# Local attention with global keys feeding a four-expert attention layer: global keys in place, finer VectorE steps, searched order

## The chip, the cores and the metric

One core of one Trainium2 chip. The metric is the device time in microseconds (us) of one execution; lower is better. The core has TensorE (PE in the profile, its weight loads PEld), VectorE (DVE), ScalarE (ACT), GpSimd (POOL) and SyncE (SP), which here only issues transfers. Every engine works through its own list of instructions in order and waits on semaphores for the others.

## The reference

Two layers follow each other, for 4 batches of 768 positions. The first is attention with 8 heads of 64 columns: a position sees the 8 global keys (positions 0 to 7) and the last 96 positions, with a bias that falls linearly with the distance. The second gives each position to 2 of 4 experts, and each expert is a causal attention head of its own.

```python
scores = scale * (q @ k.T)
is_global = pos[None, :] < 8
is_local = (rel >= 0) & (rel < 96)
dist = where(is_global & ~is_local, 96.0, abs(rel))
scores = where(is_global | is_local, scores - slopes * dist, -1e9)
x = softmax(scores) @ v            # 8 heads side by side: (4, 768, 512)

logits = x @ w_gate                # 4 experts, the best 2 are kept
w = softmax over the 2 kept logits
for e in range(4):
    a = softmax(causal(scale * (x @ wq[e]) @ (x @ wk[e]).T))
    out += w[e] * (a @ (x @ wv[e]) @ wo[e])
```

## The kernel before

**Tiling.** The work is cut into 24 row tiles ("units" u) of 128 positions: 4 batches b of 6 tiles ri. `unit(u)` adds some 35 stages per tile to a planner. R = 4 copies of most buffers go round.

**Stages of one tile.** Three loads (ldq, ldk, ldv, 256 KB each, line 537) fill `raw`. POOL casts q and k to 16 bits (cq, ck) and v into `V1` (cv). PE transposes q and k into PSUM (tq, line 554), and DVE copies them out to `qkT` (eq). For each half hf of the heads: PE forms the scores against the tile's own 128 keys and against the tile before, there for the first 96 queries only (s0, s1, line 583); ACT takes the exponential (x0, x1, line 590); the mask and bias are multiplied in on DVE or POOL (m0, m1, line 595); PE multiplies with the values (z0, z1, lines 601 to 609), whose 65th column of ones gives the sum; DVE takes its reciprocal into `rall` (line 616) and scales (line 617), both in one stage n0, n1. Then the transposed x (tx, line 649, and ex) goes through the expert weights: pq (queries and keys, line 659) and pv (values and gate, line 665), evacuated by eqk and ev. The gate is xr on ACT and wr on DVE, one stage of three instructions: the largest values `mx` (line 683), `wr` (684), and the reciprocal `zi` (686). The expert scores s2 (line 700), exponentials x2 (704), the causal cut af on POOL (712), the products y2 (724), then n2 on DVE, one stage of three instructions: reciprocal (730), weight `cw` (731), scaling (733). Then tz, ez, po (line 749), eo and the store so (758).

**Global keys before.** Once per batch POOL copies the 8 global keys of each head into a zeroed matrix `KG` (line 566, eight small copies), and builds `VG`, the global values times their bias factor (lines 436 and 439), from eight small loads (line 485). For each tile but the first of a batch, PE forms all heads' global scores in one product (sg, line 637, 4 products), ACT takes the exponential (xg, line 641), and z begins with one product of 260 columns against `VG` (line 601).

**The order.** `Stream` is a list planner that runs when the program is built. Each stage has a key, a function, the engines that could do it with a length each, the stages it follows, a rank and, for PE, a kind of PSUM slot: "s" (2 slots of two banks) or "w" (4 slots of one bank). `run()` takes at each step the stage and engine with the earliest start, ties going to the lower rank (5.0 × u plus a number per stage); a stage's second engine counts as 0.25 us later. A PSUM slot is taken in turn: stage n waits for the one that used the slot n places before. A change between products on 64 and 128 rows counts 0.1 us. The instructions are issued in the order found, so the list of each engine, SP's queue of transfers too, is fixed.

**The end.** A count of sums within a safe range is loaded as a flag (line 795), and every engine tests it (line 796): if a sum was out of range, `general_path`, a slow exact version, runs. In the usual case it is passed by. `preferred_fallthrough_block=False` places the usual case right behind the test, with a branch over the general path after it; instructions of line 828 are the program's closing waits.

Of the kernel before, what the change touches and what calls it, by code (L numbers as in the profile page):

```python
# [15 lines left out]
HUGE = 1.0e30  # L16
# [3 lines left out]
PACE = 5.0  # L20
# [219 lines left out]
class Stream:  # L240
# [4 lines left out]
    def __init__(self, kinds):  # L245
        self.free = {"PE": 0.0, "ACT": 0.0, "DVE": 0.0, "POOL": 0.0, "DMA": 0.0}
        self.tail = {"PE": 0.22, "ACT": 0.13, "DVE": 0.13, "POOL": 0.15, "DMA": 2.0}
        self.kinds = {k: (n, []) for k, n in kinds.items()}
        self.rows = False
        self.ops, self.done = {}, {}  # L250

    def add(self, key, fn, engines, after=(), rank=0.0, kind=None, until=()):


        assert key not in self.ops, key
        self.ops[key] = (fn, engines, tuple(after), rank, kind, tuple(until))

    def turn(self, e, kind):

        return 0.1 if e == "PE" and (kind == "s") != self.rows else 0.0  # L260

    def ready(self, key):
        fn, engines, after, rank, kind, until = self.ops[key]
# [5 lines left out]
        if kind:  # L269
# [4 lines left out]
            n, taken = self.kinds[kind]  # L274
            if len(taken) >= n:
                for a in taken[-n]:
                    if a not in self.done:
                        return None
                    t = max(t, self.done[a])
        return t  # L280

    def run(self):
        left = dict.fromkeys(self.ops)
        while left:
            best = None
            for key in left:
# [9 lines left out]
            start, key, e, length = best[3:]  # L296
            fn, engines, after, rank, kind, until = self.ops[key]
            if kind:
                self.kinds[kind][1].append(until)
            if e == "PE":  # L300
                self.rows = kind == "s"
# [7 lines left out]
def kernel(  # L309
# [18 lines left out]
    NL = N_G * H  # L328
# [504 lines left out]
```

## Time and profile before

| | us |
|---|---|
| median of 3 runs | 180.56 (180.41 to 185.12) |
| the profiled execution | 180.74 |
| its span, first to last instruction | 179.0 |
| mean granted TensorE clock | 0.953 |

The profile is one execution. Its page has the busy time of each engine, the span in 40 slices (of 4.475 us here), the chain of work that ended last, followed back from the last instruction, and groups of instructions with the time their engine was idle before them. A releaser is what ended an idle time. A record's length reaches to the acknowledged write, so the next independent instruction of an engine can start before it ends: the distance between two starts is what an instruction costs its engine.

### The profile page before, as it was taken

The numbers are of one execution on the slowest core, as the hardware profiler recorded it, in microseconds if no ns is written. First come the engines' busy times: TensorE is split into PE (matmuls) and PEld (weight loads), VectorE is DVE, ScalarE is ACT, GpSimd is POOL, SyncE is SP. The second block draws the span as 40 slices with busy tenths as digits, with TensorE's granted clock in tenths as the row PEclk, the third lists the DMA queues.
The fourth block names the chain that finished last, engine by engine and source line by source line (L and its number), as shares of the span: only waits on it lengthen the run. The fifth ranks groups of instructions, "written<-read, shape, count | busy, mean of one in ns | idle before, by whom it ended". The sixth has DMA issues, their size and how long they took to land.

```text
span 179.0 us, 5965 instructions
## 1 busy us (share of the span) xinstructions
PE 139.7 (78%) x2366; PEld 109.7 (61%) x2366; DVE 138.6 (77%) x438; ACT 110.2 (62%) x203; POOL 93.3 (52%) x169
## 2 busy tenths in 40 slices
PE   0447697499897889899999998987799987997510
PEld 0236585377775767678677876765697666774300
DVE  7554867978989699998989899879996897956500
ACT  3904138277675798546988567497568893279410
POOL 7566854764867448824957186899501650112000
PEclk9999669999999999999999999999999999999855
DMA  5996995999799599979899999910101031011120
GB/s 125 297 176 183 257 214 147 211 231 222 177 218 233 149 232 230 242 165 243 200 221 277 219 227 250 230 63 5 59 4 62 0 121 59 4 59 61 61 70 9
DMA packets 80693, 27.80 MB, mean 155 GB/s; under 512 B 75793, under 2 KB 77329, under 8 KB 80657
## 3 DMA queue, kind: packets, MB, share of 16 engines
q1 hardware_dynamic: 80656, 27.34, 67.6%
q8 instruction: 20, 0.33, 0.8%
q14 instruction: 17, 0.13, 0.3%
HBM read 21.05 MB, written 6.29 MB: 153 GB/s over the span
## 4 chain that ended last, share of the span: by engine, by line
DVE 44%; PE 34%; DMA 6%; ACT 4%; issue 3%; SPq 3%; ACTq 0%; DVEq 0%
DVE A L595 10%; PE pq L659 8%; DVE x L617 5%; DVE cw L731 5%; DVE qkT L347 5%; DVE z L733 4%; PE po L749 4%; PE pv L665 4%; DMA raw<-in_v_dram 4%; PE z L724 3%; DVE QK L347 3%; PE s L700 3%; PE tx L649 3%; DMA w<-in_moe_wv_dram 2%; SPq L537 2%
## 5 line engine op out<-in xcount | busy, mean ns | idle before, releaser
L704 ACT ACTIVATE A<-s 128x1024 f16<-128x1024 f32 (+1 forms) x48 | 42.2, 923 | 11.6 <-PE s L700 11.1
L590 ACT ACTIVATE A<-sc 128x896 f16<-128x896 f32 (+1 forms) x48 | 40.1, 870 | 3.1 <-PE sc L583 2.7
L347 POOL CAST qk<-raw 128x512 f16<-128x512 f32 x47 | 30.9, 670 | 15.8 <-DMA raw<-in_k_dram 8.0
L712 POOL TENSOR_SCALAR_AFFINE_SELECT A<-A 128x512 f16<-128x512 f16 x24 | 15.9, 661 | 36.0 <-ACT A L704 32.4
L595 DVE TENSOR_TENSOR A<-A,M 128x896 f16<-128x896 f16 (+1 forms) x37 | 26.1, 719 | 2.8 <-ACT A L590 2.6
L659 PE MATMUL pq<-xT,wqk 128*128 128x128 f16 x384 | 27.0, 227 | 0.4 <-DVE xT L347 0.2
L659 PEld LDWEIGHTS <-wqk 128*128 128x128 f16 x384 | 24.2, 102 | 2.1 <-issue 0.4
L595 POOL TENSOR_TENSOR A<-A,M 128x896 f16<-128x896 f16 (+1 forms) x11 | 19.9, 1806 | 5.3 <-ACT A L590 4.9
L617 DVE TENSOR_TENSOR x<-z,rall 128x256 f16<-128x256 f32 x48 | 20.4, 425 | 1.6
L347 POOL CAST V<-raw 128x512 f16<-128x512 f32 x24 | 15.3, 642 | 11.7 <-PE z L609 8.3
L554 PE MATMUL tq<-ident,qk 128*128 128x128 f16 x192 | 16.1, 230 | 5.3 <-POOL qk L347 4.9
L347 DVE CAST QK<-pq 128x512 f16<-128x512 f32 x21 | 14.4, 686 | 6.9 <-PE pq L659 6.7
L606 PE MATMUL z<-V,A 128*128 128x65 f16 x192 | 17.5, 197 | 2.6 <-DVE A L595 1.6
L347 ACT COPY o_sb<-po 128x512 f32<-128x512 f32 x18 | 10.6, 588 | 12.9 <-PE po L749 8.9
L347 ACT CAST V<-pv 128x256 f16<-128x256 f32 x23 | 8.6, 376 | 15.5 <-PE pv L665 15.4
L749 PE MATMUL po<-wo,zT 128*128 128x512 f16 x48 | 14.9, 393 | 4.0 <-DVE zT L347 3.9
L347 DVE COPY qkT<-tq 128x1024 f16<-128x1024 f16 x24 | 16.3, 684 | 2.1 <-PE tq L554 1.9
L606 PEld LDWEIGHTS <-A 128*128 128x128 f16 x192 | 14.3, 100 | 6.0 <-DVE A L595 2.6
L700 PE MATMUL s<-QK 64*128 64x128 f16 x336 | 15.3, 218 | 1.7 <-ACT A L590 1.1
L583 PE MATMUL sc<-qkT 64*128 64x128 f16 x192 | 14.6, 223 | 2.5 <-ACT A L590 1.2
L554 PEld LDWEIGHTS <-qk 128*128 128x128 f16 x192 | 12.4, 103 | 6.4 <-POOL qk L347 5.1
L665 PE MATMUL pv<-wvg,xT 128*128 128x264 f16 x96 | 15.5, 286 | 1.0 <-DVE wvg L347 1.0
(75 smaller groups left out, 263.5 us busy)
## 6 DMA issues: line engine op xcount, KB each, us to landing
raw<-in_q_dram SPq DMA_DIRECT2D x24, 256.0 KB
raw<-in_k_dram SPq DMA_DIRECT2D x24, 256.0 KB
raw<-in_v_dram SPq DMA_DIRECT2D x24, 256.0 KB
out_dram<-o_sb SPq DMA_DIRECT2D x24, 256.0 KB
w<-in_moe_wq_dram SPq DMA_DIRECT2D x1, 512.0 KB
w<-in_moe_wk_dram SPq DMA_DIRECT2D x1, 512.0 KB
w<-in_moe_wv_dram SPq DMA_DIRECT2D x1, 512.0 KB
wo<-in_moe_wo_dram SPq DMA_DIRECT2D x1, 512.0 KB
```

Source lines behind the costliest of these rows:

```text
L347: act.copy(o, i) if e == "ACT" else (dve if e == "DVE" else pool).tensor_copy(o, i)
L554: nc.tensor.transpose(ps[:, s, p, :], qk16[u % 3][:, s, 2 * p:2 * p + 2, :], ident[:, :])
L590: act.activation(A1[(2 * u + hf) % (2 * R)][:, :, :, 0:w], T.pop(("s", u, hf))[:, :, :, 0:w], func=Exp, scale=scale1)
L595: eng[e].tensor_tensor(a, a, M[:, hf, :, :, :] if ri else M0[:, hf, :, :, :], op=Alu.mult)
L606: mm(z[:, h % 4, :], lhsT=a[:, par, pr, 0:P], rhs=V1[u % (R + 1)][:, h, 0:DV], start=not ri, stop=not ri)
L617: dve.tensor_tensor(x16[i][:, 256 * hf:256 * hf + 256].rearrange("p (h d) -> p h d", d=Dh), z[:, :, 0:Dh], r.unsqueeze(2).to_broadcast([P, ...
L659: mm(ps[:, j, :], lhsT=wqk[:, ko, j, :], rhs=xT[i][:, ko, :], start=(ko == 0), stop=(ko == nko - 1))
L665: mm(ps[:, :], lhsT=xT[i][:, ko, :], rhs=wvg[:, ko, :], start=(ko == 0), stop=(ko == nko - 1))
L700: mm(sc[:, par, n, :], lhsT=QK2[b % 2][L, ki, 2 + p2, :], rhs=QK2[b % 2][L, ri, p2, :], start=True, stop=True)
L704: act.activation(A2[i][:, :, 4 * ch:4 * ch + m, :], T.pop(("s2", u, ch))[:, :, 0:m, :], func=Exp, scale=scale2)
L712: pool.affine_select(out=A2[i][:, :, 0:2, :], in_=A2[i][:, :, 0:2, :], pattern=[[0, 2], [0, 2], [1, P]], channel_multiplier=-1, base=0, co ...
L749: mm(ps[:, :], lhsT=zT[i][:, p2, :], rhs=wo[:, p2, :], start=(p2 == 0), stop=(p2 == E // 2 - 1))
```

## The change

- **Global keys in place.** A query of tile ri sees at most 95 positions back, so of the tile before it the keys 0 to 7 are never local. After tile u's own scores are done, its keys 0 to 7 in `qkT` are overwritten with the batch's global keys (kp, a small copy on POOL or DVE from the saved `KG`), and after its z products its values 0 to 7 in `V1` with the global values (vp, a transfer in SP's queue from the saved `VG`). The next tile then finds the global keys in the tile before it. The mask of the tile before covers 128 queries instead of 96, with the global distance put in by one more minimum (d1). The matrix `KG` with zeros, the products sg, the exponential xg, the eight loads, the building of `VG` and the `VG` product of z are gone. s of tile u + 1 follows kp of tile u, and z follows vp. `V1` has 4 copies instead of 5.
- **Small VectorE steps as own stages.** n0 becomes r0 and n0, n1 becomes r1 and n1; wr becomes mx, wr and zi; n2 becomes rz, cw and n2.
- **PSUM.** A stage takes any free slot, the one free the longest, and buffers are named by slot.
- **Ranks.** Cost is start + an extra per stage for its second engine (`OTHER`) + 0.000376 × rank, with searched ranks per stage (`RANK`) and for the weight loads (`W_RANK`).
- **The end.** The test has no preferred block, and one hint instruction per engine marks the branch as likely taken.

```diff
+PACE, ALPHA, TURN = 6.00622, 0.000375979, 0.1
+OTHER = {"m0": 3.12, "m1": 3.35, "eqk": 1.71, "ev": 14.02, "eo": 5.29, "kg": -15.22, "kp": 7.23}
+RANK = {
+    "ldq": 3.09, "ldk": -1.4103, "ldv": 10.549, "cq": 15.151, "ck": -10.082, "cv": -4.5336,
...
+W_RANK = -47.481, 2.337, 16.829, -53.198, 17.758
...
-            n, taken = self.kinds[kind]
-            if len(taken) >= n:
-                for a in taken[-n]:
-                    if a not in self.done:
-                        return None
-                    t = max(t, self.done[a])
+            free = [(max([self.done[a] for a in r], default=0.0), n)
+                    for n, r in enumerate(self.kinds[kind]) if all(a in self.done for a in r)]
+            if not free:
+                return None
+            when, self.slot = min(free)
+            t = max(t, when)
...
-                for n, (e, length) in enumerate(self.ops[key][1].items()):
-                    start = max(t, self.free[e] + self.turn(e, self.ops[key][4]))
-                    c = (start + (0.25 if n else 0.0), self.ops[key][3], n, start, key, e, length)
-                    if best is None or c[:3] < best[:3]:
-                        best = c
+                for n, (e, length) in enumerate(engines.items()):
+                    turn = TURN if e == "PE" and rows != self.rows else 0.0
+                    start = max(t, self.free[e] + turn)
+                    c = start + OTHER.get(stage, 0.0) * n + ALPHA * rank
+                    if best is None or c < best[0]:
+                        best = c, start, key, e, length, self.slot
...
+    st.add("d1", dmin(d[:, P:2 * P], d[:, P:2 * P]), {"DVE": 0.35}, ["mask", "dg"], rank=-16.0)
...
-        add("cv", lambda e: copy(e, V1[u % (R + 1)][:, :, 0:Dh], raw[i][:, 2, :, :]),
-            {"POOL": 0.6}, ["ldv", ("z0", u - R), ("z1", u - R), c("V1one")], 1.5)
+        add("cv", lambda e: copy(e, V1[i][:, :, 0:Dh], raw[i][:, 2, :, :]), {"POOL": 0.6},
+            ["ldv", c("V1one")] + [(n, u - R + a) for a in range(2) for n in ("z0", "z1")])
...
+            add("kg", lambda e: copy(e, KG[b % 2][:, :, :], qkT[i][:, 1, :, 0:N_G]), {"POOL": 0.12, "DVE": 0.1},
+                ["eq"] + [("kp", w) for w in range(u - 2 * n_rt, u - n_rt)])
+            add("vg", lambda e: copy(e, VG[b % 2][:, :, :], V1[i][0:N_G, :, :]), {"POOL": 0.55},
+                ["cv"] + [("vp", w) for w in range(u - 2 * n_rt, u - n_rt)])
...
-                            o = sc[:, par, pr, P:P + N_L] if prev else sc[:, par, pr, 0:P]
-                            mm(o, lhsT=kt[L, 1, p, :],
-                               rhs=qkT[i][L, 0, p, 0:N_L] if prev else qkT[i][L, 0, p, :],
+                            mm(sc[:, par, pr, prev * P:(prev + 1) * P], lhsT=kt, rhs=qkT[i][L, 0, p, :],
                                start=True, stop=True)
...
-                if ri:
-                    mm(z[:, :, :], lhsT=ag[i][:, :], rhs=VG[:, b, 4 * hf:4 * hf + 4, :],
-                       start=True, stop=False)
...
+            add(f"s{hf}", s1, {"PE": 0.24 if ri else 0.13}, ["eq"] + ([("kp", u - 1)] if ri else []),
+                None, "s", [f"x{hf}"], True)
...
+            add(f"z{hf}", z1, {"PE": 0.25 if ri else 0.13}, [f"m{hf}", "cv"] + ([("vp", u - 1)] if ri else []),
+                None, "w", [f"r{hf}", f"n{hf}"])
+            add(f"r{hf}", lambda e, hf=hf, r1=r1: dve.reciprocal(r1, T["z", u, hf][:, :, Dh]), {"DVE": 0.09},
+                [f"z{hf}"])
...
+        if ri < n_rt - 1:
+            add("kp", lambda e: copy(e, qkT[i][:, 1, :, 0:N_G], KG[b % 2][:, :, :]), {"POOL": 0.12, "DVE": 0.1},
+                [("kg", b * n_rt), "s0", "s1"])
+            add("vp", lambda e: nc.sync.dma_start(V1[i][0:N_G, :, :], VG[b % 2][:, :, :]), {"DMA": 0.1},
+                [("vg", b * n_rt), "z0", "z1"])
...
+        add("mx", lambda e: dve.max(mx[i][:, :], T["pv", u][:, lg0:lg0 + 2 * E]), {"DVE": 0.1}, ["pv", ("wr", u - R)])
...
+        add("zi", lambda e: dve.reciprocal(zi[i][:, :], zall[:, u:u + 1]), {"DVE": 0.08}, ["wr", ("cw", u - R)])
...
+        add("rz", lambda e: dve.reciprocal(r2, T["z2", u][:, :, Hd]), {"DVE": 0.09}, ["y2"])
...
+    st.add("hint", lambda e: tc.mark_branch_hint_location("general", "LikelyTaken", engines=engines),
+           {"DVE": 0.0}, [("y2", last)], PACE * NU + 30.0)
...
-    with tc.If(n_good < P * NU * (H + E + 1), preferred_fallthrough_block=False):
+    with tc.If(n_good < P * NU * (H + E + 1), label="general"):
```

## Rows read from the trace of the kernel before

**Rows 1.** Page: busy time by engine; rate in 40 slices; chain's shares.
```profile
PE 139.7 (78%) x2366; PEld 109.7 (61%) x2366; DVE 138.6 (77%) x438; ACT 110.2 (62%) x203; POOL 93.3 (52%) x169
...
GB/s 125 297 176 183 257 214 147 211 231 222 177 218 233 149 232 230 242 165 243 200 221 277 219 227 250 230 63 5 59 4 62 0 121 59 4 59 61 61 70 9
...
DVE 44%; PE 34%; DMA 6%; ACT 4%; issue 3%; SPq 3%; ACTq 0%; DVEq 0%
```

**Rows 2.** Busy us by stretch: PE, PEld, DVE, ACT, POOL; clock, DMA, GB/s.
```profile
18.00:25.00 7.00, 5.49 (x55) 4.63 (x52) 5.12 (x18) 1.82 (x4) 5.10 (x8) 0.56 1.15 244
40.00:158.00 118.00, 105.72 (x1894) 84.83 (x1888) 104.21 (x323) 81.75 (x146) 65.50 (x104) 1.00 0.70 156
80.00:100.00 20.00, 18.93 (x362) 15.31 (x361) 17.93 (x56) 16.51 (x26) 12.29 (x24) 1.00 1.05 237
158.00:171.00 13.00, 9.63 (x161) 6.06 (x158) 6.72 (x32) 9.18 (x16) 1.92 (x3) 0.92 0.17 62
```

**Rows 3.** Groups by form: busy us, mean ns of one | idle before.
```profile
L704 ACT ACTIVATE A<-s 128x1024 f16<-128x1024 f32 x36 | 35.9, 1030 | 9.8 <-PE s L700 9.4
L590 ACT ACTIVATE A<-sc 128x896 f16<-128x896 f32 x40 | 35.6, 924 | 3.1 <-PE sc L583 2.7
...
L595 POOL TENSOR_TENSOR A<-A,M 128x896 f16<-128x896 f16 x9 | 17.6, 1952 | 5.2 <-ACT A L590 4.9
...
L601 PE MATMUL z<-VG,ag 128*128 128x260 f16 x40 | 11.2, 281 | 2.1 <-DVE QK L347 1.2 <-ACT ag L641 0.5 <-DVE x L617 0.2
...
L731 DVE SCALAR_TENSOR_TENSOR cw<-wr,zi,rall 128x4 f32<-128x4 f32 x24 | 10.0, 415 | 0.9
...
L637 PE MATMUL sg<-qkT,KG 128*128 128x128 f16 x80 | 7.8, 219 | 1.1 <-DVE qkT L347 1.1
```

**Rows 4.** Chain that ended last, one piece: start us, us, what.
```profile
134.68 0.89 PE pq L659 x16
```

**Rows 5.** Instructions of DVE in order of time, around 101 us: start us, us.
```profile
100.07 0.61 DVE L595 TENSOR_TENSOR A<-A,M 128x896 f16<-128x896 f16 x1
100.60 0.17 DVE L730 RECIPROCAL rall<-z 128x4 f32<-128x4 f32 x1
100.81 0.22 DVE L731 SCALAR_TENSOR_TENSOR cw<-wr,zi,rall 128x4 f32<-128x4 f32 x1
101.07 0.42 DVE L733 TENSOR_TENSOR z<-z,cw 128x256 f16<-128x256 f32 x1
...
101.87 0.16 DVE L686 RECIPROCAL zi<-zall 128x1 f32<-128x1 f32 x1
101.95 0.67 DVE L347 CAST QK<-pq 128x512 f16<-128x512 f32 x1
```

**Rows 6.** Instructions in order of time, DVE and POOL around 31.4 us.
```profile
31.40 1.92 DVE L731 SCALAR_TENSOR_TENSOR cw<-wr,zi,rall 128x4 f32<-128x4 f32 x1
31.42 1.88 POOL L595 TENSOR_TENSOR A<-A,M 128x896 f16<-128x896 f16 x1 [0.37 <-ACT A L590]
```

**Rows 7.** Transfers issued by SP, in order of time, 9 to 14 us.
```profile
9.86 3.73 SPq L485 DMA_DIRECT2D vg<-in_v_dram  x8
13.63 0.40 SPq L471 DMA_DIRECT2D w<-in_moe_wv_dram  x1
```

**Rows 8.** Chain that ended last: a load at the start, the last copy.
```profile
6.58 6.71 DMA raw<-in_v_dram
...
170.86 0.59 ACT o_sb L347
```

**Rows 9.** Waits of SP's queue: us in total, times, longest.
```profile
SPq L758 <- ACT o_sb L347: 36.1, 12, 10.0
```

**Rows 10.** SP's instructions of lines 796 and 828: lengths, first and last start.
```profile
L796 SPq EVENT_SEMAPHORE  x8: 17/17/17, 172.5 to 174.9; - x8
...
L796 SPq COMPARE_BRANCH  x2: 37/45/53, 172.4 to 175.0; - x2
...
L828 SPq EVENT_SEMAPHORE  x10: 17/28/28, 177.7 to 179.0; - x10
```

More of the change, by code (lines that the diff above doesn't have):

```diff
@@ L246, in __init__, with add @@
         self.free = {"PE": 0.0, "ACT": 0.0, "DVE": 0.0, "POOL": 0.0, "DMA": 0.0}
-        self.tail = {"PE": 0.22, "ACT": 0.13, "DVE": 0.13, "POOL": 0.15, "DMA": 2.0}
-        self.kinds = {k: (n, []) for k, n in kinds.items()}
+        self.tail = {"PE": 0.20, "ACT": 0.15, "DVE": 0.12, "POOL": 0.10, "DMA": 2.0}
+        self.kinds = {k: [()] * n for k, n in kinds.items()}
         self.rows = False
-        self.ops, self.done = {}, {}
-    def add(self, key, fn, engines, after=(), rank=0.0, kind=None, until=()):
+        self.ops, self.done, self.slot = {}, {}, None
+    def add(self, key, fn, engines, after=(), rank=0.0, kind=None, until=(), rows=False, stage=None):
         assert key not in self.ops, key
-        self.ops[key] = (fn, engines, tuple(after), rank, kind, tuple(until))
-    def turn(self, e, kind):
-        return 0.1 if e == "PE" and (kind == "s") != self.rows else 0.0
+        self.ops[key] = (fn, engines, tuple(after), rank, kind, tuple(until), rows, stage)
     def ready(self, key):
-        fn, engines, after, rank, kind, until = self.ops[key]
+        fn, engines, after, rank, kind, until, rows, stage = self.ops[key]
         t = 0.0
@@ L455 @@
-    for hf in range(2):
-        st.add(("M", 0, hf), c_factor(True, hf), {"ACT": 0.9}, ["d0"], rank=-6)
-        st.add(("M", 1, hf), c_factor(False, hf), {"ACT": 1.2}, ["mask"], rank=2.0)
-    st.add("bmd", c_bm, {"POOL": 1.0}, rank=4.0)
-    st.add("bm", lambda e: act.activation(bm[:, :], bm[:, :], func=Exp, scale=-1.0), {"ACT": 0.15},
-           ["bmd"], rank=4.0)
-    st.add("VG0", fill([VG[:, :, :, :]], 0.0), {"DVE": 1.2, "POOL": 1.9}, rank=4.0)
-    st.add("KG0", fill([t[:, :, :] for t in KG], 0.0), {"DVE": 0.7, "POOL": 1.1}, rank=2.0)
@@ L463, with dmin @@
-    st.add("V1one", fill([t[:, :, Dh:DV] for t in V1], 1.0), {"DVE": 0.3, "POOL": 0.3}, rank=-1)
+    def dmin(o, i):
+        return lambda e: dve.tensor_tensor(o, i, dg[:, :], op=Alu.min)
+    st.add("ident", lambda e: make_identity(nc, ident[:, :]), {"POOL": 0.7}, rank=-20.0)
+    st.add("iota", c_iota, {"POOL": 0.45}, rank=-19.0)
+    st.add("d", lambda e: dve.tensor_copy(d[:, :], di[:, :]), {"DVE": 0.3}, ["iota"], rank=-19.0)
+    st.add("dg", c_dg, {"POOL": 0.45}, rank=-18.0)
+    st.add("mask", c_mask, {"POOL": 0.9}, ["d"], rank=-18.0)
@@ L467 @@
-    st.add("ones", fill([ones[:, :]], 1.0), {"DVE": 0.1}, rank=99.0)
+    st.add("ones", fill([ones[:, :]], 1.0), {"DVE": 0.1}, rank=20.0)
     def ld(o, i):
@@ L519, in unit, with add @@
         n_ch = (len(ent) + 3) // 4
[L520 to L522 removed]
+        def add(name, fn, engines, after=(), stage=None, kind=None, until=(), rows=False):
             def full(a):
[L524 to L528 removed]
+                return a[0] if isinstance(a, tuple) and a[1] is None else a if isinstance(a, tuple) else (a, u)
+            st.add((name, u), fn, engines, [x for x in map(full, after) if x in st.ops or not
+                                            (isinstance(x, tuple) and isinstance(x[1], int) and x[1] < u)],
+                   PACE * u + RANK[stage or name], kind, [full(a) for a in until], rows,
+                   stage or name)
         def c(key):
@@ L540, in unit @@
         for n, src in enumerate((q, k, v)):
-            add("ld" + "qkv"[n], load(n, src), {"DMA": 1.2}, [("c" + "qkv"[n], u - R)], -1.0 + 0.1 * n)
+            add("ld" + "qkv"[n], load(n, src), {"DMA": 1.2}, [("c" + "qkv"[n], u - R)])
         for n in range(2):
@@ L630, in unit @@
[L630 to L642 removed]
+                               rhs=V1[(u - 1) % R][:, h, 0:DV], start=False, stop=True)
@@ L693, in unit @@
             m = len(part)
+            first = "" if ch == 0 else "+"
             def s2(e, ch=ch, part=part):
```

230 lines of the change are left out of this document (81 added, 149 removed), and 7 rows, old and new, of the table RANK.

## Prediction

> **What bounds the kernel now.** I read the page's busy shares and chain first. TensorE (PE) is busy 78% of the span, VectorE (DVE) 77%, ScalarE (ACT) 62%, GpSimd (POOL) 52%, and the chain that ended last is 44% DVE and 34% PE [rows 1]: two engines hand the work to each other, and neither can be shortened alone. The busy table by stretch then splits the span into four regimes [rows 2]. Up to about 25 us the pipeline fills while data arrive; in 18 to 25 us the granted clock is 0.56, so TensorE ran mostly at the lower of its two levels (1.2 and 2.4 GHz). From 40 to 158 us, 118 us, PE is busy 105.7 us (90%) and DVE 104.2 us (88%). From 158 to 171 us the last row tiles drain, PE at 9.6 of 13 us. The best 20 us (80 to 100) have PE at 18.93, or 95%: PE can nearly be filled. After the last copy, at 171.4 us [rows 8], nothing computes, yet the span goes on to 179.0 [rows 10]. So a gain comes from less PE work, from less DVE work where DVE is what PE waits for, and from the two ends.
>
> All sums are against the profiled execution: 180.74 us, a span of 179.0 and 1.7 around it. The median of the runs, 180.56, lies 0.2 below; I treat them as equal.
>
> **The end (branch and hint).** The SyncE queue (SP) meets the test of the flag at 172.4, walks eight semaphore waits from 172.5 to 174.9 (the last store's landing is among them), meets a second branch at 175.0, and the first instruction behind it starts at 177.7 [rows 10]: 2.7 us in which it waits for nothing but its next instructions. The last stretch takes 177.7 to 179.0. The change drops the order "general path out of line", so the usual case leaves by one taken branch at the test, and hints it. If the hint works, the jump is free, the waits end at 174.9 as before, and 1.3 us follow: −2.7. If the hint does nothing, the same 2.7 us stall starts at 172.4 and ends at 175.1, now beside the store's landing; the eight waits, all met by then, cost at most the 0.13 us apiece of line 828 (ten in 1.3 us), I count 0.6, and 1.3 follow: end 177.0, −2.0. The hint instructions, one per engine, have no row; the nearest are SP's branches of 37 to 53 ns, so nothing to 0.1. I take −2.7.
>
> The Trainium skill, "Runtime: NRT & Kernel Launch", section "Instruction fetch mechanics", speaks for the lower value: instructions are held in two lines that are refilled in sequence, and a taken branch outside them must fetch first. By that rule a target fetched early may be gone again, and the sum ends 0.7 us higher. The 2.7 us behind the old jump agrees with the stall; no run before shows a hinted branch.
>
> **PE work.** Gone are the scores against the collected global keys, 80 products of 128 columns (L637), and 40 products of 260 columns for their values (L601) [rows 3]. A row's mean (219 ns) is the length of one in a pipeline, so I price columns: 16 products of 128 columns take 0.89 us back to back [rows 4], 0.056 each. L637: 80 × 0.056 = 4.5 us. L601: 40 × 0.056 × 260/128 = 4.5 us. Added: the previous tile's scores grow from 96 to 128 columns, 160 products × 0.014 = 2.2 us. Net −6.8 us of PE, spread over 20 of 24 row tiles. Where PE is the bound this is time saved one for one; where DVE is, it becomes idle PE. Bounds: −6.8 and 0. I take all of it, because PE is the busier engine in the stretch.
>
> **DVE work.** The small steps become pieces that the planner may put between others. In the trace a dependent pair starts 0.21 us apart (rall to cw) or 0.26 (cw to z), an independent one 0.08 (zi to QK) [rows 5]. Per row tile there are five dependent pairs (two r to n, mx to wr, rz to cw, cw to n2), so 120 × 0.13 = 15.6 us at most, none at least; I take half, −7.8. The new price for leaving DVE (over 3 us for the masks m0 and m1, 0.25 before) brings most of POOL's nine wide masks (1952 ns each) [rows 3] back: 9 × 0.53 × 1024/896 = +5.5 us on DVE (start distance 0.53, 1024 columns instead of 896) [rows 5]. The other 31 wide masks grow by 0.08 each: +2.4. Against that, POOL masks block DVE: a cw beside one took 1.92 us, the mask 1.88 [rows 6], and an undisturbed one 0.22 [rows 5]; cw's mean is 415 ns [rows 3], so 24 × 0.19 = −4.7. Sum −4.6, between −12.4 (all 15.6 recovered) and +7.9 (neither overlap nor relief).
>
> **What that is worth.** PE is idle 12.3 of the 118 us; at the best stretch's 95% it would idle 6.3. So freer slots in PSUM, pieces and ranks can give 0 to −6 beyond the PE work. Half: −3.
>
> **ACT and POOL.** The wide exponential goes from 896 to 1024 elements: 1030 − 924 = 0.106 us × 40 = +4.2 us; the 20 small ones of the global scores leave. ACT stays near 62%: nothing. POOL loses the masks and the building of the global values and gains 20 small copies kp; at 52% it hides them. Without this cover, a late kp holds the next tile's scores.
>
> **The front.** SP issued eight small loads for the global values from 9.86 to 13.59 and the weights wv only at 13.63 [rows 7]. They go: −3.7 at most for what is behind. But the searched order (rank 6.0 × tile + the stage's rank, weights −47.5 and 2.3) puts two weights of 512 KB ahead of the first q, so the first tile has its q and k after 1.5 MB instead of 0.5 MB: at the some 200 GB/s of the first slices [rows 1], 5 us later. TensorE does little there, and the bytes that must come before full speed stay the same. Between +5 and −3.7; I take −1, nearer to the freed issue time because that hole is seen and the delay falls where PE waits anyway.
>
> **The new waits.** Each vp is a transfer in SP's queue that waits for both z of its tile, 20 in all, with later loads behind it, and the next tile's z waits for its landing. A row tile takes (171 − 18)/24 = 6.4 us. A landing took 6.7 us from the start of issue with a full queue [rows 8] and at most 3.5 us (last copy at 171.4, end of the waits at 174.9) [rows 8, 10] when nothing else was under way. I count nothing: the chain runs only within a batch, and loads end near 116 us, where the rate falls to a store's (slice 26 of 40) [rows 1].
>
> The Trainium skill, "DMA: Bandwidth & Descriptors", section "Queues, rings and completion order", says that each DMA engine takes a ring's descriptors in order; by it a tiny vp lands behind every load issued before it. The 6.7 us agrees. This is rival 3.
>
> **Sum.** 180.7 − 2.7 − 6.8 − 3 − 1 = 167.2 us.
>
> **Rivals.**
> 1. Everything closes up: front −3.7, idle −6: 180.7 − 2.7 − 6.8 − 6 − 3.7 = 161.5; without the slow clock of 18 to 25 us (0.44 × 7 = 3.1 us) 158.4. For it: DVE's −12.4 is possible. Against: 95% was reached in one stretch only.
> 2. DVE becomes the bound: the pieces don't overlap, the masks come back, DVE work rises by up to 7.9, and PE's loss becomes idle time. Then only the two ends are left: 180.7 − 2.7 − 1 = 177.0, with DVE's rise up to 181. For it: DVE is at 88% and leads the chain.
> 3. Slower: vp sets the pace. With 6.7 us to land and 0.5 for z (16 products of 65 columns at the rate of the pq products) [rows 4], a step takes 7.2 us against 6.4 − 0.4 = 6.0 in the forecast; it decides from a landing above 5.5 us. If loads keep their time, 12 of the 20 steps meet a full queue: 12 × 1.2 = 14.4, so 181.7. But a waiting vp holds the loads behind it (SP's store waits for ACT alone already add up to 36.1 us [rows 9]), the queue stays full to the end, and all 20 pay: 24, so 191. Between them some 186.
> 4. The end doesn't do what it says: two jumps as before, 169.9; or the hint alone is dead, 167.9. Both inside the forecast's own range.
>
> **How the numbers follow.** Forecast with rival 4, 163.5 to 173: 0.58. Rival 1: 0.20. Rival 2: 0.16, three quarters of it within 2%. Rival 3: 0.06. A measurement here tells about 2%, so faster means below 177.0. Faster: 0.58 + 0.20 + 0.04 = 0.82; same 0.12; slower 0.06. The range reaches into rivals 1 and 2: 159.5 to 177.
>
> **What would show it.** Right: on SP one branch, no 2.7 us hole, under 6 us from the last copy to the end; no L637 or L601 rows; about 133 us of PE busy; cw means near 0.25 us; dependent small steps with another instruction between; POOL masks down to a few; the first TensorE work near 9 us; PE at 92% or more in the middle. Wrong: DVE above 92% in the middle with PE below 88% (rival 2); z waiting for a transfer into V, or SP's waits for z growing (rival 3). The forecast fails above all if the middle's pace stays at 6.4 us a row tile.

## The result and the profile after

The changed kernel takes 157.35 us (median of 4 runs, 156.72 to 157.88); the kernel before, beside it on the same chip, 181.69 us. The ratio is 0.868, interval 0.859 to 0.877. Some executions of a kernel run over 1.5% longer than its fastest at a lower granted clock; ratios, and the times of the runs below, leave them out. The prediction was 167.2 us with a range from 159.5: faster, as forecast, but by some 24 us where it had 13.5, and outside the range.

The page of the changed kernel, busy time by engine and the chain's shares:

```profile
PE 124.4 (80%) x2246; PEld 99.6 (64%) x2246; DVE 126.7 (81%) x438; ACT 111.0 (71%) x186; POOL 72.0 (46%) x132
...
PE 35%; DVE 21%; DMA 20%; POOL 6%; ACT 5%; issue 5%; SPq 4%; POOLq 0%; ACTq 0%; DVEq 0%
```

Against [rows 1] the span is 23.2 us shorter (179.0 to 155.8). TensorE's busy time falls by 15.3 us and its idle time by 7.9 (39.3 to 31.4). VectorE's share of the chain falls from 44 to 21%, and that of the transfers rises from 6 to 20%. By the starts of the pq products in the two traces, the fifth row tile comes 6.2 us earlier (41.6, 47.8 before), the way from it to the last tile takes 96.6 us instead of 110.9 (5.1 and 5.8 a tile), and what follows takes 17.6 instead of 20.3. By stretch:

```profile
18.00:25.00 7.00, 6.08 (x83) 5.19 (x80) 5.40 (x14) 3.77 (x7) 2.24 (x4) 1.00 0.79 231
40.00:140.00 100.00, 92.67 (x1761) 75.63 (x1762) 93.34 (x318) 81.79 (x130) 53.20 (x91) 1.00 0.80 178
80.00:100.00 20.00, 19.10 (x383) 15.66 (x378) 19.50 (x64) 16.87 (x27) 11.60 (x19) 1.00 0.98 226
140.00:151.00 11.00, 8.42 (x134) 5.12 (x132) 6.78 (x39) 8.15 (x16) 0.64 (x1) 0.98 0.43 156
```

In the middle TensorE is at 93% (90% in [rows 2]), VectorE too. The granted clock of 18 to 25 us is full where it was 0.56. Groups of instructions:

```profile
L563 ACT ACTIVATE A<-sc 128x1024 f16<-128x1024 f32 x40 | 40.2, 1034 | 10.5 <-PE sc L559 10.3
L568 DVE TENSOR_TENSOR A<-A,M 128x1024 f16<-128x1024 f16 x40 | 28.9, 730 | 1.0 <-ACT A L563 0.9
...
L592 DVE TENSOR_TENSOR x<-z,rall 128x256 f16<-128x256 f32 x48 | 19.2, 412 | 0.0
L358 DVE CAST QK<-pq 128x512 f16<-128x512 f32 x24 | 16.3, 680 | 1.6 <-PE pq L618 1.6
...
L689 DVE SCALAR_TENSOR_TENSOR cw<-wr,zi,rall 128x4 f32<-128x4 f32 x24 | 7.3, 303 | 0.1
...
L644 DVE RECIPROCAL zi<-zall 128x1 f32<-128x1 f32 x24 | 3.5, 150 | 0.1
```

All 40 wide masks are on VectorE (9 were on POOL [rows 3]), cw's mean fell from 415 to 303 ns, and the groups L601 and L637 of [rows 3] are gone. The idle time of TensorE ahead of three stages that wait for VectorE has gone as well. The same groups, before and then after:

```profile
L749 PE MATMUL po<-wo,zT 128*128 128x512 f16 x48 | 14.9, 393 | 4.0 <-DVE zT L347 3.9
L649 PE MATMUL tx<-ident,x 128*128 128x128 f16 x96 | 10.2, 231 | 3.6 <-DVE x L617 3.1 <-ACT A L704 0.2
L744 PE MATMUL tz<-ident,z 128*128 128x128 f16 x48 | 7.0, 229 | 6.8 <-DVE z L733 6.3
```

```profile
L536 PE MATMUL tq<-ident,qk 128*128 128x128 f16 x192 | 16.1, 231 | 16.3 <-POOL qk L358 15.8 <-DVE wr L641 0.3 <-DVE z L692 0.2
L705 PE MATMUL po<-wo,zT 128*128 128x512 f16 x48 | 14.3, 380 | 0.3 <-DVE zT L358 0.2
L608 PE MATMUL tx<-ident,x 128*128 128x128 f16 x96 | 9.8, 225 | 0.9 <-DVE x L592 0.6
L700 PE MATMUL tz<-ident,z 128*128 128x128 f16 x48 | 6.7, 221 | 0.6 <-DVE z L692 0.6
```

14.4 us of waiting became 1.8. What TensorE waits for now is tq, for casts of loaded rows (10.4 of its 16.3 us are the start of the program). The small steps stand between others now, VectorE in order of time:

```profile
94.80 0.17 DVE L590 RECIPROCAL rall<-z 128x4 f32<-128x4 f32 x1
94.89 0.39 DVE L592 TENSOR_TENSOR x<-z,rall 128x256 f16<-128x256 f32 x1
95.20 0.16 DVE L640 MAX8 mx<-pv 128x8 f32<-128x8 f32 x1
95.28 0.40 DVE L592 TENSOR_TENSOR x<-z,rall 128x256 f16<-128x256 f32 x1
```

The instruction behind the reciprocal starts 0.09 us after it, where a dependent one took 0.21 to 0.26 [rows 5]; its half isn't named in the row, but by that distance it is the scaling of the other half. At the end, the branch of each engine's sequencer and what follows (line 757: first and last start):

```profile
L757 SPq EVENT_SEMAPHORE  x8: 17/17/17, 153.8 to 154.4; - x8
L757 POOLq COMPARE_BRANCH  x1: 65/65/65, 149.4 to 149.4; - x1
...
L757 DVEq COMPARE_BRANCH  x1: 89/89/89, 149.5 to 149.5; - x1
L757 ACTq COMPARE_BRANCH  x1: 68/68/68, 149.8 to 149.8; - x1
...
L757 POOLq EVENT_SEMAPHORE  x1: 17/17/17, 149.9 to 149.9; - x1
L757 DVEq EVENT_SEMAPHORE  x1: 21/21/21, 150.1 to 150.1; - x1
L757 ACTq EVENT_SEMAPHORE  x1: 17/17/17, 150.2 to 150.2; - x1
L757 SPq COMPARE_BRANCH  x1: 70/70/70, 150.8 to 150.8; - x1
```

SyncE has one branch, at 150.8, and goes on at 153.8. That is the wait for the store: its last part lands at 153.81 by the trace, and in all 12 kernels here that have this hint SyncE goes on at that landing, 2.1 to 3.1 us after its branch. From landing to end 1.95 us remain, where 4.35 were (174.69 to 179.04, with the second branch between [rows 10]). The landing itself came 4.0 us after the last copy, 3.25 before, so 1.6 us of the total come from the end and 21.6 from ahead of the last copy (171.44 to 149.81).

### The profile page after: what moved, and what is told of

It is laid out like the page before. It is cut to its first block, busy times and chain, and to the rows that moved or that the text cites. A ratio compares the mean times of both kernels' runs of the same rounds, so it can differ in the third digit from the quotient of the medians.

```text
span 155.8 us, 5666 instructions
## 1 busy us (share of the span) xinstructions
PE 124.4 (80%) x2246; PEld 99.6 (64%) x2246; DVE 126.7 (81%) x438; ACT 111.0 (71%) x186; POOL 72.0 (46%) x132
## 4 chain that ended last, share of the span: by engine, by line
PE 35%; DVE 21%; DMA 20%; POOL 6%; ACT 5%; issue 5%; SPq 4%; POOLq 0%; ACTq 0%; DVEq 0%
DMA raw<-in_q_dram 13%; DMA raw<-in_k_dram 7%; PE pq L618 6%; DVE A L568 5%; POOL qk L358 5%; PE tq L536 5%; PE po L705 4%; PE z L682 4%; PE s L658 4%; DVE qkT L358 4%; PE pv L624 3%; ACT A L563 3%; PE sc L559 3%; DVE QK L358 2%; DVE cw L689 2%
## 5 line engine op out<-in xcount | busy, mean ns | idle before, releaser
L563 ACT ACTIVATE A<-sc 128x1024 f16<-128x1024 f32 (+1 forms) x48 | 44.8, 962 | 16.0 <-PE sc L559 15.8
L662 ACT ACTIVATE A<-s 128x1024 f16<-128x1024 f32 (+1 forms) x48 | 44.0, 929 | 9.1 <-PE s L658 9.0
L358 POOL CAST qk<-raw 128x512 f16<-128x512 f32 x47 | 31.4, 671 | 31.2 <-DMA raw<-in_q_dram 19.2
L568 DVE TENSOR_TENSOR A<-A,M 128x1024 f16<-128x1024 f16 (+1 forms) x48 | 32.8, 690 | 1.6 <-ACT A L563 1.4
L536 PE MATMUL tq<-ident,qk 128*128 128x128 f16 x192 | 16.1, 231 | 16.3 <-POOL qk L358 15.8
L618 PE MATMUL pq<-xT,wqk 128*128 128x128 f16 x384 | 26.2, 223 | 0.9 <-DVE xT L358 0.7
L670 POOL TENSOR_SCALAR_AFFINE_SELECT A<-A 128x512 f16<-128x512 f16 x24 | 16.8, 699 | 18.8 <-ACT A L662 17.7
L618 PEld LDWEIGHTS <-wqk 128*128 128x128 f16 x384 | 23.1, 100 | 2.6 <-issue 0.9
L358 DVE COPY qkT<-tq 128x1024 f16<-128x1024 f16 x24 | 16.3, 678 | 4.1 <-PE tq L536 3.9
L576 PE MATMUL z<-V,A 128*128 128x65 f16 x192 | 17.7, 198 | 2.3 <-POOL V L358 0.9
L592 DVE TENSOR_TENSOR x<-z,rall 128x256 f16<-128x256 f32 x48 | 19.2, 412 | 0.0
L358 DVE CAST QK<-pq 128x512 f16<-128x512 f32 x24 | 16.3, 680 | 1.6 <-PE pq L618 1.6
L358 ACT COPY o_sb<-po 128x512 f32<-128x512 f32 x24 | 14.4, 606 | 2.2 <-PE po L705 1.3
L579 PE MATMUL z<-V,A 128*128 128x65 f16 x160 | 14.9, 195 | 0.1
L559 PEld LDWEIGHTS <-qkT 64*128 64x128 f16 x352 | 10.9, 97 | 5.9 <-issue 2.8
```

What stands on the lines that cost most here:

```text
L358: act.copy(o, i) if e == "ACT" else (dve if e == "DVE" else pool).tensor_copy(o, i)
L536: nc.tensor.transpose(ps[:, s, p, :], qk16[u % 3][:, s, 2 * p:2 * p + 2, :], ident[:, :])
L559: mm(sc[:, par, pr, prev * P:(prev + 1) * P], lhsT=kt, rhs=qkT[i][L, 0, p, :], start=True, stop=True)
L563: act.activation(A1[(2 * u + hf) % (2 * R)][:, :, :, 0:w], T.pop(("s", u, hf))[:, :, :, 0:w], func=Exp, scale=scale1)
L568: eng[e].tensor_tensor(a, a, M[:, hf, :, :, :] if ri else M0[:, hf, :, :, :], op=Alu.mult)
L576: mm(z[:, h % 4, :], lhsT=a[:, par, pr, 0:P], rhs=V1[i][:, h, 0:DV], start=True, stop=not ri)
```

## The experiments

The parts: G, global keys in place; V, small VectorE steps as pieces; P, any free PSUM slot; O, the values of OTHER, which bring the masks back from POOL; R, the searched ranks; H, the end. Three sets: one part undone and all planned anew; one part undone with the changed kernel's order kept; and the parts added one by one under the old ranks. Ratios are to the kernel before on the same chip.

### One part alone, and parts undone and planned anew

**e7_keys_only**: G alone. The diff is the change's own, backwards, for all else.

> Of the change this kernel keeps only the global keys in place (KG, VG, kp, vp); the small VectorE steps are merged again (r+n, mx+wr+zi, rz+cw+n2), PSUM slots go in turn, the ranks, weights' ranks, pace and OTHER are the old ones, and the end is the old one without hint. By the prediction's sum this part alone is the 6.8 us of TensorE work, less the wide masks' 2.4 us on VectorE where that is the bound: 174 to 177 us. Theory D (VectorE is what TensorE waits for, so freed TensorE time turns into idle time): 178 to 181. Theory Q (the transfers vp sit in the queue between the loads and hold the next tile): above 181.

Measured: 187.5 us, ratio 1.041 (1.031 to 1.051). Alone, the central edit makes the kernel slower. POOL now has 17 masks (11 before), and cw's mean is 615 ns.

**e3_old_ranks**: R undone.

```diff
-PACE, ALPHA, TURN = 6.00622, 0.000375979, 0.1
+PACE, ALPHA, TURN = 5.0, 1.0e-6, 0.1
-W_RANK = -47.481, 2.337, 16.829, -53.198, 17.758
+W_RANK = 1.0, 1.5, 6.0, 6.0, 12.0
```

and the stages' ranks of the kernel before.

> The changed kernel with the old ranks within a tile, the old ranks of the weights, pace 5.0 and alpha 1e-6; the values of OTHER stay the new ones. Theory O (the order from the search makes the unforeseen gain of some 10 us: it keeps TensorE fed and packs the last row tiles): 164 to 170 us, TensorE's work after 140 us spread over some 13 us as before. Theory V (the pieces and the masks brought back from POOL make it): 157 to 160. The prediction's own sum gives the ranks a third of 3 us: 158 to 159.

Measured: 167.5 us, 0.930 (0.920 to 0.940). Without the searched order the kernel loses some 10 us, as theory O has it; PE is busy 131.6 us for the same 2246 products that took 124.4.

**e4_old_other**: O undone.

```diff
-OTHER = {"m0": 3.12, "m1": 3.35, "eqk": 1.71, "ev": 14.02, "eo": 5.29, "kg": -15.22, "kp": 7.23}
+OTHER = {"m0": 0.25, "m1": 0.25, "eqk": 0.25, "ev": 0.25, "eo": 0.25, "kg": 0.25, "kp": 0.25}
```

> The changed kernel with every value of OTHER at 0.25, so that wide masks go to POOL again. Theory L (POOL's masks block VectorE, cw beside one took 1.92 us against 0.22, and their absence is what the prediction undersized): 161 to 166 us, cw's mean back above 400 ns. Theory O (the order makes the gain): 157 to 159. The prediction's sum, +5.5 on VectorE for the masks brought back against -4.7 of relief, gives no difference: 157 to 158.

Measured: 167.4 us, 0.930 (0.921 to 0.938), beyond both theories.

**e1_merged**: V undone (n0 = r0 and n0 in one stage, and so on).

> The changed kernel with the small VectorE steps merged into stages again: r+n, mx+wr+zi, rz+cw+n2 each issued back to back, all else as changed. Theory V (pieces overlap and their 0.09 us starts in place of 0.21 are the gain): 120 dependent pairs by 0.12 are 14 us of VectorE, of which at 80% busy at least half shows: 163 to 167 us. The prediction's sum (half of -3): 158 to 160. Theory O: 157 to 160, too.

Measured: 171.6 us, beyond both. Its page:

```profile
PE 128.3 (76%) x2246; PEld 99.4 (59%) x2246; DVE 136.9 (81%) x436; ACT 111.5 (66%) x186; POOL 77.0 (45%) x134
```

Each of the three parts undone costs 10 to 14 us, some 34 in all, more than the whole gain: planning anew spoils the order too, so these runs don't price a part.

### Parts undone in the changed kernel's own order

Here the rest can't adapt to what is undone, so a loss is what the part is worth to this order. Such losses overlap as well: those of this set add up to over 40 us.

**f1_order_merged**: every stage at its place, but r issued in n's stage, mx and zi in wr's, rz and cw in n2's.

```diff
-            add(f"r{hf}", lambda e, hf=hf, r1=r1: dve.reciprocal(r1, T["z", u, hf][:, :, Dh]), {"DVE": 0.09},
+            add(f"r{hf}", lambda e: None, {"DVE": 0.09}, [f"z{hf}"])
```

> The changed kernel with its planned order kept for every stage, but each small VectorE step issued directly in front of (or, for zi, behind) the big one it belongs to, as in the old stages. Only the interleaving of the pieces is gone, the order is not planned anew. Theory V (the pieces overlap and save 0.12 us in each of up to 120 dependent pairs, that is the surplus): 163 to 170 us. Theory O (planning the merged stages with ranks that were searched for pieces made e1_merged slow, 173.4): 158 to 162.

Measured: 166.2 us, 0.916 (0.907 to 0.925): undoing the pieces costs 8.8 us, theory V. VectorE's instructions of this kernel in order of time:

```profile
98.71 0.17 DVE L699 RECIPROCAL rall<-z 128x4 f32<-128x4 f32 x1
98.92 0.22 DVE L700 SCALAR_TENSOR_TENSOR cw<-wr,zi,rall 128x4 f32<-128x4 f32 x1
99.18 0.42 DVE L702 TENSOR_TENSOR z<-z,cw 128x256 f16<-128x256 f32 x1
```

The old distances of 0.21 and 0.26 us are back. Its page:

```profile
PE 129.5 (78%) x2246; PEld 100.8 (61%) x2246; DVE 138.0 (83%) x438; ACT 111.7 (67%) x186; POOL 73.0 (44%) x132
```

VectorE's busy time grows by 11.3 us, and TensorE's by 5.1 with not one product more (granted clock 0.978, 0.983 after).

**f2_order_pool**: the 11 masks of e4_old_other on POOL, all else in place.

```diff
-                eng[e].tensor_tensor(a, a, M[:, hf, :, :, :] if ri else M0[:, hf, :, :, :], op=Alu.mult)
+                eng["POOL" if (u, hf) in ON_POOL else e].tensor_tensor(
+                    a, a, M[:, hf, :, :, :] if ri else M0[:, hf, :, :, :], op=Alu.mult)
```

> The changed kernel with its planned order kept, but the same 11 wide masks on POOL that e4_old_other put there. Theory L (a mask on POOL takes 2 us instead of 0.73, and slows VectorE beside it): each of the 11 comes 1.3 us later to z, and VectorE loses 0.2 to 1 us at each: 161 to 168 us, as e4_old_other's 169.6. Theory O (e4_old_other lost by another order): 157 to 160.

Measured: 166.7 us, 0.919 (0.911 to 0.927): 9.3 us, theory L. VectorE's groups:

```profile
L569 DVE TENSOR_TENSOR A<-A,M 128x1024 f16<-128x1024 f16 x29 | 26.9, 930 | 1.6 <-ACT A L564 1.6
L594 DVE TENSOR_TENSOR x<-z,rall 128x256 f16<-128x256 f32 x48 | 19.1, 410 | 0.0
L359 DVE CAST QK<-pq 128x512 f16<-128x512 f32 x24 | 16.3, 679 | 1.5 <-PE pq L620 1.4
...
L691 DVE SCALAR_TENSOR_TENSOR cw<-wr,zi,rall 128x4 f32<-128x4 f32 x24 | 9.7, 406 | 0.1
...
L646 DVE RECIPROCAL zi<-zall 128x1 f32<-128x1 f32 x24 | 3.4, 148 | 0.1
```

With 11 masks fewer VectorE is busy for 130.0 us, 3.3 more: the masks left to it take 930 ns (730 after), cw 406 (303). Both read several tiles, all in SBUF. What reads PSUM (x, QK) keeps its time, and so does zi, which reads one tile in SBUF (148, 150).

**f3_order_products**: the old products' columns put back, overwritten by the real ones.

```diff
+                if ri:
+                    for x in range(2):
+                        mm(sc[:, 0, x, 0:P], lhsT=qkT[(u - 1) % R][0:Dh, 1, 2 * hf + x, :],
+                           rhs=qkT[i][0:Dh, 0, 2 * hf + x, :], start=True, stop=True)
```

and one of 260 columns ahead of each z.

> The changed kernel with its planned order kept, and the TensorE columns of the old global keys put back as extra products: 80 of 128 columns and 40 of 260, overwritten by the real ones, 9.0 us at 0.056 us per 128 columns. If TensorE is the bound in the middle, as the prediction took it, 164 to 168 us; if the space is hidden behind the loads (front to 116 us) or VectorE, 158 to 162.

Measured: 161.8 us, 0.894 (0.885 to 0.904): 4.4 us for 9.0 us of columns (an estimate at 0.056 us per 128), between the two expectations. About half of TensorE's work shows.

**p_order_turn**: P undone.

```diff
+                    if len(taken) >= size and any(a not in done for a in taken[-size]):
+                        continue
+                    self.slot = len(taken) % size
```

> The changed kernel in its planned order, but with PSUM slots taken in turn. In the plan 150 of 217 tiles of the kind w do not take the slot that is next in turn; 17 could not have it without waiting for a reader that stands later, and only these move behind their next ready stage. Theory F (taking whichever slot is free is a large part of the gain, since a slot in turn waits for the slowest of four): 163 to 170 us. The prediction's sum, a third of 3 us: 158 to 160.

Measured: 177.3 us, 0.988 (0.980 to 0.996): 20 us, most of the gain, and more than any theory had. TensorE's waits in this kernel (in total, times, longest):

```profile
PE z L593 <- ACT V L375: 2.2, 1, 2.2
PE tx L625 <- DVE qkT L375: 2.0, 2, 1.4
PE pq L635 <- DVE z L709: 1.7, 2, 0.9
...
PE pq L635 <- ACT V L375: 1.3, 1, 1.3
```

None of these is a wait for data: this z reads the values that POOL cast, not the projected ones that ACT copies, tx doesn't read qkT, nor pq what VectorE writes to z. Each releaser is the reader of another PSUM tile, the one that held the slot. 17 stages also stand later than in the changed order, so the number is for both. The mean granted clock of this profile is 0.954 (0.983 after), so by estimate up to 0.03 of its 178 us, some 5 us, are the clock's.

**q_first** and **q_first_again**: the first tile's k and q ahead of the weights, all else in order (`first = [("ldk", 0), ("ldq", 0)]`, moved to the head of the plan). Expected of q_first was 156.5 to 158 us, 152.5 to 155 if the late first q runs through to the end, and 158 to 160 if the later weights are missed. Its four runs took 155.6 to 160.7, too wide to tell, so the same kernel ran again:

> The kernel of q_first once more, whose four runs spread from 155.6 to 160.7. If the earlier first q and k are worth something: fast runs at 154 to 156, and a ratio below 0.86. If they fall where TensorE waits anyway: 156.5 to 158.5, ratio 0.865 to 0.875, like the changed kernel's.

Measured: 157.2 us, 0.873 (0.867 to 0.879). The first transposes start at 6.0 us, not 10.4, and nothing comes of it.

### The end

**e5_old_end**: H undone.

```diff
-    with tc.If(n_good < P * NU * (H + E + 1), label="general"):
+    with tc.If(n_good < P * NU * (H + E + 1), preferred_fallthrough_block=False):
```

> The changed kernel without the hint and with the old order of blocks (general path out of line), all else the same. The end is then two branches: 2.7 us behind the second one, after the wait for the last store. By the two profiles (last copy to the end of the span 7.55 us before, 6.0 after) +1.5 us: 158.5 to 160, with the 2.7 us hole in SyncE's list again. If the end was worth nothing: 157 to 158.

Measured: 160.7 us, 0.892 (0.886 to 0.897). The second branch and its hole are back:

```profile
L752 SPq COMPARE_BRANCH  x2: 38/44/49, 155.9 to 158.9; - x2
...
L784 SPq EVENT_SEMAPHORE  x10: 17/28/28, 161.6 to 163.1; - x10
```

From landing to end there are 4.90 us (158.30 to 163.20) where the changed kernel has 1.95: 2.95 us, of the 3.3 between the medians. The jump over the general path holds the other engines up too: by the trace ScalarE's next instruction starts 2.8 us behind its second branch and VectorE's 3.3, TensorE's branch is 3.4 us long, and POOL goes on after 0.15.

**h3_late_hint**: the plan in two blocks, the hint at the second's start.

```diff
+    with tc.block():
+        with tc.manual_schedule():
+            st.run(("y2", last))
+    tc.mark_branch_hint_location("general", "LikelyTaken", engines=engines)
```

> The changed kernel with the plan cut into two blocks behind the last y2, so that the hint instruction stands at the start of the second block, some 10 us before the branch, instead of at the program's first microsecond. If a hint that is alive takes SyncE's 3.0 us stall behind the branch away, the end is bound by the last store's landing and the time is 0.5 to 2 us shorter: 155 to 157 us. If the hint does nothing here either: 157 to 158.5. The unconditional branch between the blocks costs 0.05 us per engine, or, if it too has to fetch, up to 3 us on TensorE: 160.

Measured: 157.55 us, 0.869 (0.862 to 0.876), no difference. The expectation had misread SyncE's 3.0 us, which are the store's landing, and taken the early hint for dead. The branch line of this kernel says otherwise:

```profile
L762 DVEq COMPARE_BRANCH  x1: 89/89/89, 150.4 to 150.4; - x1
...
L762 ACTq COMPARE_BRANCH  x1: 68/68/68, 151.0 to 151.0; - x1
...
L762 SPq COMPARE_BRANCH  x1: 70/70/70, 152.0 to 152.0; - x1
L762 ACTq EVENT_SEMAPHORE  x1: 17/17/17, 154.6 to 154.6; - x1
L762 DVEq EVENT_SEMAPHORE  x1: 21/21/21, 154.7 to 154.7; - x1
```

With the hint at the program's start ACT goes on 0.5 us after its branch and VectorE 0.6; with a hint some 3 to 5 us ahead they wait 3.6 and 4.2, and SyncE goes on at 155.06, 0.7 us after its landing at 154.37. POOL and TensorE go on after 0.5 and 1.5. So the early hint is the one that goes with short jumps, on ScalarE, VectorE and TensorE against e5's unhinted ones too. On SyncE it need not show: by e5's 2.7 us, a stall behind its branch at 150.9 would end at 153.6, still before the landing. One kernel lands early enough to tell, e3:

```profile
L755 SPq EVENT_SEMAPHORE  x8: 17/17/17, 165.8 to 166.4; - x8
...
L755 SPq COMPARE_BRANCH  x1: 70/70/70, 163.7 to 163.7; - x1
```

There SyncE goes on 2.15 us after its branch, at the landing (165.82), so its stall was below 2.2 us. What the hint is worth by itself wasn't tried, as no kernel has the one branch without a hint.

### Parts added under the old order

**b1_before_masks**: the kernel before in its order, its 11 POOL masks on VectorE (`dve.tensor_tensor` in m1).

> The kernel before in its own planned order, but with its 11 POOL masks (9 of 896 columns, 2 of 512) issued on VectorE; nothing else is changed. Theory L (masks on POOL slow VectorE and come late, worth some 9 us in f2_order_pool): 171 to 177 us although VectorE gets 11 instructions more. The prediction's account (+4.7 us of VectorE work against 4.7 of relief): 179 to 182. If VectorE is the bound and the lock is small: 183 to 186.

Measured: 178.9 us, 0.992 (0.988 to 0.997).

```profile
L731 DVE SCALAR_TENSOR_TENSOR cw<-wr,zi,rall 128x4 f32<-128x4 f32 x24 | 6.3, 260 | 0.9
```

cw's mean falls to 260 ns, VectorE's busy time by 2.2 us with 11 masks more, and the kernel gains 1.4: in the old order the masks are worth far less than the 9.3 us of f2.

**c1_before_order_free**: the kernel before in its order, slots by who is free first.

```diff
+                self.slot = min((max([self.done[a] for a in r], default=0.0), n)
+                                for n, r in enumerate(self.hold[kind]) if all(a in self.done for a in r))[1]
```

> The kernel before in its own planned order, with one difference: each PSUM tile takes the slot whose last reader ends first by the plan, not the next in turn. Theory F1 (slots in turn held the old kernel up by themselves): 160 to 172 us. Theory F2 (free slots only allow another order; an order planned for turns gains little from them): 177 to 181.

Measured: 180.6 us, 1.008 (0.993 to 1.023): no gain, theory F2.

**c3_keys_free** (e7 and P) and **c4_keys_free_masks** (and O):

> e7_keys_only (global keys in place, everything else old: 189.5 us) with free slots in the plan as the only addition; masks may go to POOL, small steps merged, old ranks, old end. Theory F1 (free slots are worth some 20 us, as p_order_turn lost): 166 to 176. Theory F2 (they are worth that only with an order searched for them): 181 to 189.

> c3_keys_free with the masks kept on VectorE (new values of OTHER), small steps still merged, old ranks, old end. From c3 to here is what the masks are worth with the old ranks, from here to e3_old_ranks (169.0) what the pieces and the end are. If masks and pieces share as they did in the fixed order (9.3 and 8.8 us): about 178 to 181. If VectorE with merged steps and all masks is too full to gain: 184 to 190.

Measured: 193.8 us, 1.081 (1.062 to 1.100), and 179.0, 0.998 (0.967 to 1.030). In c3 the planner puts 19 masks on POOL:

```profile
L566 POOL TENSOR_TENSOR A<-A,M 128x1024 f16<-128x1024 f16 x14 | 30.1, 2150 | 10.8 <-ACT A L561 10.6
...
L696 DVE SCALAR_TENSOR_TENSOR cw<-wr,zi,rall 128x4 f32<-128x4 f32 x24 | 20.7, 862 | 0.9
```

In c4, with none, cw's mean is 260. With the old ranks the ladder reads: before 180; G 187.5; with P 193.8; with O 179.0; with V and H 167.5; with R 157.35. Without the ban on POOL masks, G and P make the kernel slower; O then takes some 15 us (c4's interval is 6 us to either side), V and H 11.5, R 10. Another sequence of adding would share the gain out otherwise.

### What bounds the changed kernel

**d1_half_loads**:

```diff
+            hs = slice(0, H if u < R else H // 2)
```

> The changed kernel in its order, with the loads of q, k and v cut to half the heads from the fifth row tile on (the other heads keep the data of an earlier tile, so the sums are over other numbers): some 7.9 MB of 18.9 less. If the transfers bound the first 100 us of the changed kernel (their engines are busy for 0.9 to 1.0 of each stretch): 140 to 150 us. If the chain of TensorE and VectorE does: 155 to 158.

Measured: 154.4 us, 0.861 (0.850 to 0.872); the changed kernel's 0.868 (0.859 to 0.877) overlaps. From 40 to 100 us, first the changed kernel, then this one:

```profile
40.00:100.00 60.00, 54.82 (x1057) 45.04 (x1058) 56.87 (x188) 49.02 (x77) 37.31 (x63) 1.00 0.99 214
```

```profile
40.00:100.00 60.00, 56.95 (x1074) 46.16 (x1071) 58.99 (x190) 50.34 (x78) 38.68 (x66) 1.00 0.53 131
```

The transfers' share falls from 0.99 to 0.53, and TensorE and VectorE each gain 2 us of work in these 60: the halved bytes are worth 1 us by the ratios and 3 by the medians, though the transfer engines looked full. What remains is TensorE at 95% and VectorE at 98%; which of the two bounds the other was not tried.

**s4_searched**: new values for RANK, W_RANK, OTHER and ALPHA.

> The changed kernel with other values of RANK, W_RANK, OTHER and ALPHA, found by a random search over the planner's orders in which every stage's length was stretched by a few per cent at random, so that the order has to bear lengths that are not as planned. If order is what is left to gain: 153 to 156 us. If the changed order is already at what its engines allow within what such a search sees: 156 to 160.

Measured: 158.4 us, 0.878 (0.873 to 0.883): this search found nothing better. No complete version here beats the changed kernel clearly.

## Why the prediction was right and wrong

- **The end, −2.7: right in mechanism.** One branch, no hole: landing to end shrank by 2.4 us, between the two cases (−2.7 hinted, −2.0 not): all eight waits stand behind the landing now, 0.6 us. The total gained 1.6, because the landing came 0.75 us later after the last copy. "Under 6 us from the last copy to the end" came out as 5.95. The rule of the Trainium skill ("Runtime: NRT & Kernel Launch", "Instruction fetch mechanics"), that a taken branch must first fetch, agrees with e5's 2.7 us. That a target fetched early may be gone again was not seen: with the hint at 0.8 us the jumps stayed short.
- **PE work, −6.8: over-sized.** "I take all of it": the columns are gone, but in f3 9.0 us of them cost 4.4. The same share of −6.8 is −3.3 (an estimate).
- **"What that is worth", −3 from 0 to −6: the step that failed.** Of the 21.6 us ahead of the last copy some 18 remain for pieces, masks, slots and ranks. The bound of 6 came from TensorE's idle time, at a best share of 95%. That share was nearly met (93%), and the idle time that went is near what the sum had (7.9 us over the span, 2.7 + 3 + 1 = 6.7 in the sum); but the step took busy time as work that stays, and only the 6.8 us of columns were to go from it. It fell by 15.3, so the missing 8.5 us are busy time. By the prediction's own measure a row tile takes (149.8 − 18)/24 = 5.5 us, 6.0 in the forecast and 6.4 before. Busy time moves without the work: the same 2246 products are busy for 124.4 us in the changed kernel, 128.3 in e1, 129.5 in f1 and 131.6 in e3, at nearly the same granted clock (0.983, 0.986, 0.978, 0.978). The products are no slower, pq's start 0.056 us apart in the median in all four traces. But starts more than 0.25 us apart are 46, 69, 70 and 72. A record is some 0.22 us long and most products take 0.056 or less in a run, so by estimate each such break adds 0.17 us of busy time, 3.9 to 4.4 us in these kernels: the rise in e1, most of it in f1, over half in e3. So part of what the profile counts as busy is waiting, and pieces and order removed some of it. The kernel before has 67 such breaks; the 21 fewer give 3.6 of the 8.5 us, and what gave the rest stays open.
- **DVE work, −4.6 within −12.4 to +7.9: the far end came true.** Busy time fell 11.9 us. The masks cost +6.6 (26.2 to 32.8 us in both widths), near the 7.9 of the forecast. The pieces gave 11.3 by f1, not half of 15.6. The relief from POOL was priced at cw alone; f2 shows that the other masks pay too, and most. Not priced at all were 6 copies of o_sb that went to ACT, 4.1 us, so the nearness to −12.4 is partly luck; and of the −4.6 the sum used nothing but what the −3 stands for.
- **Slots and ranks: never priced apart.** They were lumped into the −3. The runs show why neither has a price alone: free slots give nothing to an order planned for turns (c1) nor to one planned anew under the old ranks with POOL masks (c3), and taking them from an order planned for them costs 20 us.
- **The front, −1: half tried.** The later first q costs nothing (q_first_again), as the reasoning had it that the delay falls where TensorE waits. The 3.7 us of freed issue time has no run; the first pq comes 3.7 us later than before (17.3, 13.6) and the fifth tile's 6.2 earlier, for which pieces and order count too.
- **ACT and POOL at nothing: right**; ACT is at 71%, and no wait in TensorE's list names POOL's copies into qkT (kp).
- **Rivals.** Rival 1 named the outcome: 158.4 with the full clock from 18 to 25 us, which the profile shows. It had 0.20, and the range stopped at 159.5, above it. But it came there by another split: it let some 12 us of idle time go (2.7 + 6 + 3.7), where 7.9 went, and no busy time beyond the columns and the clock. So its nearness is in good part luck, and its argument against, 95% in one stretch only, was the same mistake. The clock is not the main cause: in b1 it was full there as well, and the kernel took 178.9 us with TensorE busy for 139.6. Rival 2 (177 to 181; with the whole of its +7.9 it would reach 184.9) fits no run of the whole change, but c4 (179.0) lies where its conditions put it: masks back, no pieces. Rival 3 (vp) didn't show: no wait of TensorE for a transfer into V stands in the changed kernel's list. By the trace a vp lands 1.8 to 4.0 us after its issue, never 6.7, which was the time of a 256 KB load; and 7 of the 20 land before a load that was issued ahead of them, so the ring's order does not put a vp behind all of these. Whether e7's slowness is partly vp, whose waits for TensorE hold later loads in SP's queue, stays open beside its POOL masks.
- **The signs that it named.** One branch, 5.95 us from copy to end, no L637 or L601, no POOL masks and 93% in the middle came true; TensorE's busy time (124.4 for 133), cw (303 ns for 250) and the first TensorE work (10.4 us for 9) came out otherwise.

## What to carry to other kernels

Don't bound a gain by the idle share of the busiest engine: where two engines hand work back and forth, its busy time can hold short waits too, and shrink when they go. Price an engine that slows another at every group that gets longer beside it, not at the one where it was noticed. An order and the resources that it was planned for go together: undo a part with the order kept, and add it under the old order, before you say what it is worth.

## What the hardware showed beyond that

- Masks on POOL (2.0 to 2.2 us each) lengthen those VectorE instructions that read several tiles, all in SBUF (with 11 of them masks take 930 ns for 730 and cw 406 for 303; with 19 cw takes 862, 260 in c4). They leave alone what reads PSUM (x 412 and 410, QK 680 and 679) and zi, which reads one SBUF tile (150 and 148).
- With a branch hint issued 149 us ahead, four engines took 0.4 to 0.6 us from branch to next instruction; with one issued 3 to 5 us ahead two of them took 3.6 and 4.2. Without one (e5) ScalarE, VectorE and TensorE took 2.8 to 3.4. Hinting later was worse, not better.
- Transfer engines that are 0.99 busy need not be the bound: at 0.53 the kernel was 1 to 3 us faster.
- A transfer of 8 KB issued behind loads in the same queue can land before one of them: 7 of the 20 vp did, and all 20 landed 1.8 to 4.0 us after their issue.
